# A long convolution and two MLPs in one kernel: matmuls cut into row and column tiles, and the hand-over between two stages rearranged

## The chip, the cores and the metric

The kernel runs on one core of a Trainium2 chip. A core has five engines with an instruction stream each: TensorE (PE: matmuls, and PEld: loads of the stationary operand), VectorE (DVE), ScalarE (ACT), GpSimd (POOL) and SyncE (SP). Transfers are issued from the queues of SP and ACT and run on the core's 16 DMA engines. The metric is device time in microseconds (us); of several runs the median counts.

## The reference

The input has 12480 positions and 128 channels. An implicit long convolution comes first, then two MLPs of width 2048, all in fp32:

```
h  = max(pos_emb @ w1, 0) @ w2 * exp(-0.01 * pos)     # filter, 64 -> 64 -> 128
u  = x * v
y  = irfft(rfft(u, 2S) * rfft(h, 2S), 2S)[:S]          # causal convolution over S = 12480
x1 = x * y
x2 = max(x1 @ w_in, 0)**2 @ w_out                      # first MLP
x3 = silu-like(x2 @ w_in2) @ w_out2                    # second: h * sigmoid(1.702 h)
```

## The kernel before

The Fourier transforms are matmuls with constant matrices; 12573 = 99 x 127 points are worked as 99 rows by 127. Four stages follow one another on TensorE:

- **Filter stage** (`filter_stage`): pos_emb times a block-diagonal w1, to `h`.
- **S1** (`s1_step`, L259): 48 steps of a first transform, 16 for `h` (result `G`, written to DRAM as `gd`) and 32 for `u` (result `A`, kept in SBUF). Each step has 8 matmuls whose stationary operand has 64 columns; the two halves of the output go to partitions 0 to 63 and 64 to 127.
- **S2** (`stage_s2`, L285): 99 frequencies k, in pairs p, two pairs to a group g. For a group `features` makes `fk` (4 matmuls), which ACT copies to `fs`. For a pair `spectra` makes `hk` = filter spectrum (L316: `fs` times `w2b`, a block-diagonal 128 x 256 copy of w2, 2 matmuls) and `xk` = input spectrum (L318, 2 matmuls), and ACT copies `hk` to `hc`. `product` multiplies them as complex numbers on DVE (two products `t`, L329, and a subtraction, L334) and POOL (an addition, L333). `back` transforms the product (`ob`, L342, 2 matmuls); ACT copies it to `bs` and writes it to DRAM as `bd`.
- **MLP** (`mlp`, L413): 25 tiles of up to 504 positions, 8 units to a tile and layer, 400 units in all. `unit_in` is 6 fp32r matmuls (`hin`), ACT and DVE apply the activation and split it into a high and a low part (`gh`, `gl`), and `unit_out`, four units later (LAG), is 6 matmuls (`acc`). Ahead of a tile's units its inverse transform is made: `load_b` fetches `uv` from `bd`, `combine` (L391) adds or subtracts its halves to `b`, `inverse` (L441) makes 10 matmuls into `yps`, `front_y` multiplies with x, and `split` (L428) makes `hi` and `lo`.

The weights arrive as fp64 and are converted on the chip to a high and a low fp32r part: `conversion` (L121) is 8 DVE instructions and one ACT cast for a chunk of 512 columns, and `Weights.tick` issues one step of each running conversion at a time. Of the first MLP's 8 chunks, six are converted during S2; the last two (3 and 7) are fetched near its end (ticks 44 and 46) and converted by `finish` after the last pair. The second MLP's 8 chunks are converted in the first 45 or so units.

The order of the instructions is the order in which the code is written; every engine works its own list in order. Between S2 and the first unit TensorE runs `spare`: matmuls whose result nobody reads, 9 ahead of the first tile's inverse and 2 behind it. An fp32 matmul is two records in the trace (two load and matmul pairs), an fp32r matmul is one.

Of the kernel before, what the change touches and what calls it, by code (L numbers as in the profile page):

```python
# [9 lines left out]
FP32 = mybir.dt.float32  # L10
# [4 lines left out]
ALU = mybir.AluOpType  # L15
# [12 lines left out]
D = 128  # L28
# [63 lines left out]
def conv_mlp_kernel(ctx: ExitStack, tc: tile.TileContext, xc, xt, vc, pt, w1, w2,  # L92
# [62 lines left out]
    class Weights:  # L155
# [16 lines left out]
                self.run.append(conversion(n, self.raw.pop(n), self.pool))  # L172
                next(self.run[-1])

        def finish(self):
            while self.run or self.plan:
                self.tick(1 << 30)

    class Inputs:

# [104 lines left out]
    def stage_s2(sp, mp, A, w2b, hooks, work):  # L285


        kp = tc.tile_pool(name="kp", bufs=2, space=PSUM, reuse_waits="tile")
        obp = tc.tile_pool(name="obp", bufs=2, space=PSUM, reuse_waits="tile")
        P_t, k_t, bs_t, f_t = {}, {}, {}, {}  # L290

        def pair(p):
            return min(2, N1 - 2 * p)

        with kp as kp, obp as obp:
            def features(g):


                if g >= NFK:
                    return  # L300
                n = min(FK, N1 - g * FK)
                ps = kp.tile([128, FK, 128], FP32, tag="fk", name="fk", bufs=1)
                for i in range(n):
                    k = g * FK + i
                    nc.tensor.matmul(out=ps[:, i], lhsT=h_t[k // HL][:, k % HL, :],  # L305
                                     rhs=m_t[k // 2][:, k % 2, 0, :])
                f_t[g] = sp.tile([128, FK, 128], FP32, tag="fs", name="fs", bufs=2)
                nc.scalar.copy(out=f_t[g][:, 0:n], in_=ps[:, 0:n])

            def spectra(p):  # L310
                n, m = pair(p), m_t[p]
                xk = kp.tile([128, 2, 2, D], FP32, tag="xk", name="xk", bufs=3)
                hk = kp.tile([128, 2, 2, D], FP32, tag="hk", name="hk", bufs=2)
                for j in range(n):
                    k = 2 * p + j
                    nc.tensor.matmul(out=hk[:, j], lhsT=f_t[k // FK][:, k % FK, :], rhs=w2b)  # L316
                for j in range(n):
                    nc.tensor.matmul(out=xk[:, j], lhsT=m[:, j, 0, :], rhs=A[:, 2 * p + j])  # L318
                hc = sp.tile([128, 2, 2, D], FP32, tag="hc", name="hc", bufs=2)
                nc.scalar.copy(out=hc[:, 0:n], in_=hk[:, 0:n])  # L320
                k_t[p] = xk, hc

            def product(p):
                n = pair(p)
                xk, hc = k_t.pop(p)
                t = []
                for c in range(2):
                    t.append(sp.tile([128, 2, 2, D], FP32, tag=f"t{c}", name=f"t{c}", bufs=2))
                    nc.vector.tensor_tensor(  # L329
                        out=t[c][:, 0:n], in0=xk[:, 0:n, c].unsqueeze(2).to_broadcast([128, n, 2, D]),  # L330
                        in1=hc[:, 0:n], op=ALU.mult)
                P = sp.tile([128, 2, 2, D], FP32, tag="P", name="P", bufs=3)
                nc.gpsimd.tensor_tensor(out=P[:, 0:n, 1], in0=t[0][:, 0:n, 1], in1=t[1][:, 0:n, 0], op=ALU.add)  # L333
                nc.vector.tensor_tensor(out=P[:, 0:n, 0], in0=t[0][:, 0:n, 0], in1=t[1][:, 0:n, 1],  # L334
                                        op=ALU.subtract)
                P_t[p] = P

            def back(p):
                n, m, P = pair(p), m_t.pop(p), P_t.pop(p)
                ob = obp.tile([128, 2, 2, D], FP32, tag="ob", name="ob")  # L340
                for j in range(n):
                    nc.tensor.matmul(out=ob[:, j], lhsT=m[:, j, 1, :], rhs=P[:, j])  # L342
                g, o = divmod(2 * p, HK)
                if o == 0:
                    bs_t[g] = sp.tile([128, HK, 2, D], FP32, tag="bs", name="bs", bufs=2)
                nc.scalar.copy(out=bs_t[g][:, o:o + n], in_=ob[:, 0:n])
                if o + n == HK or p == NP - 1:
# [48 lines left out]
    def load_b(bp, t):  # L396


        last = max(p[0] for p in whole(t)) // JG
        for k in range(loaded[0], last + 1):  # L400
            uv = bp.tile([N1, 2, JG, 2, D], FP32, tag="uv", name="uv", bufs=2)
            for h in range(2):
                queue = nc.scalar if t == 0 and h else nc.sync
                queue.dma_start(out=uv[:, h], in_=bd[h, k * JG:(k + 1) * JG].rearrange("j k c d -> k j c d"))
# [8 lines left out]
    def mlp(lp, cp):  # L413
# [68 lines left out]
        def front_x(t):  # L482
            split(y_t.pop(t), 0, t)
# [66 lines left out]
        for q in range(NQ + SHIFT):  # L550
            if q < NQ:
                seq.append((0, q // PAIRS, q % PAIRS))
            if q >= SHIFT:
                seq.append((1, (q - SHIFT) // PAIRS, (q - SHIFT) % PAIRS))
        for k, s, c, engine in ((0, 0, 0, nc.vector), (0, 1, 0, nc.gpsimd), (0, 0, 1, nc.vector),
                                (0, 1, 1, nc.gpsimd), (1, 0, 0, nc.vector), (1, 1, 1, nc.gpsimd),
                                (1, 0, 1, nc.vector), (1, 1, 0, nc.vector)):
            combine(k, s, c, engine)

        def spare(n):  # L560

# [2 lines left out]
                nc.tensor.matmul(out=ps[0:N1, 0:width(0)], lhsT=ci2[:, 0, :], rhs=xs[0:N1])  # L564

        xs = x_t[0][:, 0:width(0)]
        spare(9)
        front_y(0)
        spare(2)
        front_x(0)  # L570
        load_rest()
        prev = None
        work = Weights([8, 12, 9, 13, 10, 14, 11, 15], 3, 5, 3, cp)
        for n in range(len(seq) + LAG):
            work.tick(n)
            if n >= LAG:
                unit_out(*seq[n - LAG])
            if n < len(seq):
                l, t, j = seq[n]
                un = unit_in(l, t, j)  # L580
                if prev:
                    high(prev)
                gate(un)
                if prev:
                    low(prev)
                prev = un
                if l == 0:
                    if j == 0 and t + 1 < NTILE:
                        load_x(lp, t + 1)
                        load_b(bp, t + 1)  # L590
                    late = t >= SHIFT // PAIRS
                    if t == 0 and j == 2:
                        front_rest()
                    if j == 3 + late and t + 1 < NTILE:
                        front_y(t + 1)
                    if j == 5 + late and t + 1 < NTILE:
                        front_x(t + 1)
            elif prev:
                high(prev)
                low(prev)  # L600
                prev = None
        es.close()

    with tc.manual_schedule():
# [32 lines left out]
        with tc.tile_pool(name="A", bufs=1, reuse_waits="tile") as ap_, ExitStack() as mps:  # L637
            A = ap_.tile([128, N1, 2, D], FP32, name="A")
            for d in range(0, D, 4):
# [7 lines left out]
                if d // 4 == 22:  # L647
                    assert inputs.done == NXC
                    vps.close()
                    mp = mps.enter_context(tc.tile_pool(name="mh", bufs=1, reuse_waits="tile"))  # L650
                    w2b = mp.tile([128, 2 * D], FP32, name="w2b")
# [18 lines left out]
        mlp(lp, cp)  # L670


def _constants():
# [86 lines left out]
```

## Time and profile before

| | |
|---|---|
| median of 3 runs | 1419.97 us (1417.61 to 1421.13) |
| the profiled execution | 1419.01 us, span 1417.2 us, granted clock 0.993 of full |
| PE busy | 1399.3 us, 99% of the span |
| DVE, ACT, POOL busy | 1114.3 us (79%), 940.4 us (66%), 221.2 us (16%) |
| on the chain that ended last | PE 92%, DVE 4% |

The span runs from the first to the last instruction; 1.8 us lie around it. In rows of a timeline and of the chain the first number is the start in us, the second the duration in us. A matmul record's duration is modelled and longer than the distance to the next matmul, so that distance is read from the chain of waits, where a piece is as long as the engine took for it. In groups of instructions a row gives the line, engine, operation, names and shapes (for a matmul rows*columns of the stationary operand first), the count, busy us, mean ns of one, and idle time before it with what ended it. In a table of stretches the columns are the stretch, its length, busy us and count of PE, PEld, DVE, ACT and POOL, the granted TensorE clock (1.00 is 2.4 GHz, 0.50 is 1.2 GHz), the DMA engines' busy share and GB/s.

### The profile page before, as it was taken

The numbers are of one execution on the slowest core, as the hardware profiler recorded it, in microseconds if no ns is written. First come the engines' busy times: TensorE is split into PE (matmuls) and PEld (weight loads), VectorE is DVE, ScalarE is ACT, GpSimd is POOL, SyncE is SP. The second block draws the span as 40 slices with busy tenths as digits, with TensorE's granted clock in tenths as the row PEclk, the third lists the DMA queues.
The fourth block names the chain that finished last, engine by engine and source line by source line (L and its number), as shares of the span: only waits on it lengthen the run. The fifth ranks groups of instructions, "written<-read, shape, count | busy, mean of one in ns | idle before, by whom it ended". The sixth has DMA issues, their size and how long they took to land.

```text
span 1417.2 us, 17764 instructions
## 1 busy us (share of the span) xinstructions
PE 1399.3 (99%) x7018; PEld 1175.7 (83%) x7018; DVE 1114.3 (79%) x1233; ACT 940.4 (66%) x1066; POOL 221.2 (16%) x209
## 2 busy tenths in 40 slices
PE   7999999999999999999999999999999999999998
PEld 7888888788788888888888888888888888888887
DVE  7558988699887777777778777777778787777887
ACT  1654544577667767776767767777777767777776
POOL 3012222425620111111100211012101120000000
PEclk9999999899999999999999999999999999999999
DMA  9977765312200001000010000010000100000000
GB/s 248 302 247 241 242 229 195 102 60 79 68 20 8 26 20 38 25 9 20 27 38 8 27 20 26 8 38 19 27 27 8 38 19 8 8 8 1 15 15 15
DMA packets 46400, 91.34 MB, mean 64 GB/s; under 512 B 4183, under 2 KB 30604, under 8 KB 45804
## 3 DMA queue, kind: packets, MB, share of 16 engines
q1 hardware_dynamic: 36750, 64.71, 15.2%
q10 hardware_dynamic: 9566, 25.49, 4.7%
q8 instruction: 55, 0.90, 0.3%
q14 instruction: 29, 0.24, 0.1%
HBM read 64.33 MB, written 25.85 MB: 64 GB/s over the span
## 4 chain that ended last, share of the span: by engine, by line
PE 92%; DVE 4%; issue 1%; DMA 1%; ACT 1%; POOL 0%; SPq 0%; DVEq 0%; POOLq 0%; ACTq 0%
PE hin L489 12%; PE hin L490 12%; PE hin L488 12%; PE acc L489 12%; PE acc L488 12%; PE acc L490 12%; PE s L266 5%; PE yps L446 4%; PE hk L316 3%; PE xk L318 3%; PE ob L342 3%; PE fk L305 2%; DVE gl L526 1%; DVE r L250 1%; DMA uv<-bd 1%
## 5 line engine op out<-in xcount | busy, mean ns | idle before, releaser
L526 DVE TENSOR_TENSOR gl<-g,gh 128x1004 fp32r<-128x1004 f32 (+4 forms) x400 | 491.7, 1229 | 34.9 <-ACT gh L522 34.5
L506 ACT ACTIVATE g<-hin 128x1004 f32<-128x1004 f32 (+4 forms) x200 | 201.2, 1006 | 238.4 <-PE hin L490 237.9
L488 PE MATMUL acc<-gh,w 128*128 128x502 f32 (+4 forms) x800 | 313.6, 392 | 0.3 <-DVE lo L435 0.3
L488 PE MATMUL hin<-hi,w 128*128 128x502 f32 (+4 forms) x800 | 312.8, 391 | 0.0
L489 PE MATMUL acc<-gl,w 128*128 128x502 f32 (+4 forms) x800 | 311.8, 390 | 0.8 <-DVE gl L526 0.8
L489 PE MATMUL hin<-lo,w 128*128 128x502 f32 (+4 forms) x800 | 312.5, 391 | 0.0
L490 PE MATMUL hin<-hi,w 128*128 128x502 f32 (+4 forms) x800 | 311.9, 390 | 0.0
L490 PE MATMUL acc<-gh,w 128*128 128x502 f32 (+4 forms) x800 | 311.7, 390 | 0.0
L517 DVE TENSOR_TENSOR g<-hin,g 128x1004 f32<-128x1004 f32 (+4 forms) x200 | 238.7, 1193 | 50.6 <-ACT g L509 50.5
L393 POOL TENSOR_TENSOR b<-uv 99x256 f32<-99x256 f32 x127 | 158.1, 1274 | 698.4 <-DMA uv<-bd 501.0
L515 DVE CAST gh<-g 128x1004 fp32r<-128x1004 f32 (+4 forms) x200 | 142.4, 712 | 149.7 <-ACT g L507 149.6
L509 ACT ACTIVATE g<-hin 128x1004 f32<-128x1004 f32 (+4 forms) x200 | 200.1, 1001 | 75.2 <-PE hin L490 67.2
L507 ACT ACTIVATE g<-g 128x1004 f32<-128x1004 f32 (+4 forms) x200 | 208.0, 1040 | 6.4
L522 ACT CAST gh<-g 128x1004 fp32r<-128x1004 f32 (+4 forms) x200 | 202.8, 1014 | 0.4 <-DVE g L517 0.4
L488 PEld LDWEIGHTS hin<-hi,w 128*128 128x128 f32 x800 | 151.4, 189 | 33.8 <-ACT g L506 2.5
L489 PEld LDWEIGHTS acc<-gl,w 128*128 128x128 f32 x800 | 151.1, 189 | 32.0 <-DVE gl L526 2.1
L490 PEld LDWEIGHTS hin<-hi,w 128*128 128x128 f32 x800 | 151.4, 189 | 30.7
L488 PEld LDWEIGHTS acc<-gh,w 128*128 128x128 f32 x800 | 151.2, 189 | 30.8 <-DVE lo L435 0.7
L489 PEld LDWEIGHTS hin<-lo,w 128*128 128x128 f32 x800 | 151.3, 189 | 30.6 <-issue 0.5
L490 PEld LDWEIGHTS acc<-gh,w 128*128 128x128 f32 x800 | 150.8, 189 | 30.4
L329 DVE TENSOR_TENSOR t<-xk,hc 128x512 f32<-128x512 f32 (+1 forms) x100 | 63.8, 679 | 23.7 <-PE xk L318 19.5
L333 POOL TENSOR_TENSOR P<-t,t 128x256 f32<-128x256 f32 (+1 forms) x50 | 43.8, 876 | 176.8 <-DVE t L329 94.5
(56 smaller groups left out, 1032.1 us busy)
## 6 DMA issues: line engine op xcount, KB each, us to landing
uv<-bd SPq DMA_DIRECT2D x64, 198.0 KB
m<-in_c_s_dram SPq DMA_DIRECT2D x49, 256.0 KB
bd<-bs ACTq DMA_DIRECT2D x24, 512.0 KB
x<-in_xc_dram SPq DMA_DIRECT2D x16, 384.0 KB
v<-in_vc_dram SPq DMA_DIRECT2D x16, 384.0 KB
Gs<-gd ACTq DMA_DIRECT2D x10, 512.0 KB
gd<-G SPq DMA_DIRECT2D x3, 1600.0 KB
raw<-in_moe_w_in_dram SPq DMA_DIRECT2D x8, 512.0 KB
```

The source lines that it names most:

```text
L266: nc.tensor.matmul(out=ps[j, e], lhsT=src[:, d + e, j], rhs=cs1[:, half])
L393: engine.tensor_tensor(out=b[:, :, s, c], in0=uv[:, 0, :, c], in1=uv[:, 1, :, 1 - c], op=ALU.add if s != c else ALU.subtract)
L488: nc.tensor.matmul(out=out, lhsT=a, rhs=hl[0], start=first, stop=False)
L489: nc.tensor.matmul(out=out, lhsT=a, rhs=hl[1], start=False, stop=False)
L490: nc.tensor.matmul(out=out, lhsT=b, rhs=hl[0], start=False, stop=last)
L506: nc.scalar.activation(out=g, in_=ps, func=ACTF.Relu)
L507: nc.scalar.activation(out=g, in_=g, func=ACTF.Square)
L509: nc.scalar.activation(out=g, in_=ps, func=ACTF.Sigmoid, scale=1.702)
L515: nc.vector.tensor_copy(out=gh, in_=g)
L517: nc.vector.tensor_tensor(out=g, in0=ps, in1=g, op=ALU.mult)
L522: nc.scalar.copy(out=gh, in_=g)
L526: nc.vector.tensor_tensor(out=gl, in0=g, in1=gh.bitcast(FP32), op=ALU.subtract)
```

## The change

- **Row tiles in S2.** `w2` comes as two copies of its 64 rows, one above the other, instead of block-diagonal. A new function `filters` makes a whole group's `hk`: for each of 4 frequencies two matmuls with 64 rows each, one on partitions 0 to 63, one on 64 to 127, 128 columns wide, into two banks. One ACT copy of 128 x 1024 takes the place of two of 128 x 512, and in `product` one DVE multiplication of 128 x 1024 that of two of 128 x 512. `P` has two buffers instead of three.
- **Column tiles in the inverse.** Each matmul of `inverse` is cut into two with 64 columns of `b` each, into partitions 0 to 63 and 64 to 127.
- **The hand-over.** All four `uv` loads of the first tile are issued by SP (two were by ACT). The six `combine`s that tile 0 needs all run on DVE, in the order in which they are used (five were on DVE, three on POOL); the two that tile 1 needs follow on POOL behind `front_x(0)`. `spare` runs 7 instead of 9. `finish(1)` leaves one chunk (7) unconverted, and the MLP's loop converts it, one step a unit (`rest.tick`).

The diff, cut to its core (the slicing of the copies in `product` and of `w2`'s layout on the host are left out):

```
         def finish(self, left=0):
-            while self.run or self.plan:
-                self.tick(1 << 30)
+            while self.run or len(self.plan) > left:
+                self.tick(1 << 30 if len(self.plan) > left else 0)
...
+            def filters(g):
+                n = min(FK, N1 - g * FK)
+                hk = kp.tile([128, 2, FK, D], FP32, tag="hk", name="hk", bufs=1)
+                for i in range(n):
+                    for c in range(2):
+                        f = slice(c * F, (c + 1) * F)
+                        nc.tensor.matmul(out=hk[:, c, i], lhsT=f_t[g][f, i, :], rhs=w2b[f])
+                h_c[g] = sp.tile([128, FK, 2, D], FP32, tag="hc", name="hc", bufs=2)
+                nc.scalar.copy(out=h_c[g][:, 0:n], in_=hk[:, :, 0:n].rearrange("p c k d -> p k c d"))
...
-                for j in range(n):
-                    k = 2 * p + j
-                    nc.tensor.matmul(out=hk[:, j], lhsT=f_t[k // FK][:, k % FK, :], rhs=w2b)
...
+                nc.vector.tensor_tensor(out=t[:, 0:n], in0=xk[:, 0:n].unsqueeze(3).to_broadcast(full),
+                                        in1=hc.unsqueeze(2).to_broadcast(full), op=ALU.mult)
...
             for p in range(NP + 2):
+                if p < NP and p % 2 == 0:
+                    filters(p // 2)
                 if p < NP:
                     spectra(p)
...
-            work.finish()
+            work.finish(1)
...
-                queue = nc.scalar if t == 0 and h else nc.sync
-                queue.dma_start(out=uv[:, h], ...
+                nc.sync.dma_start(out=uv[:, h], ...
...
                 for c in range(2):
-                    nc.tensor.matmul(out=ps[:, o:o + w], lhsT=b[:, c, :], rhs=ci2[:, c, r:r + w],
-                                     start=(c == 0), stop=(c == 1))
+                    for d in (slice(0, D // 2), slice(D // 2, D)):
+                        nc.tensor.matmul(out=ps[d, o:o + w], lhsT=b[:, c, d], rhs=ci2[:, c, r:r + w],
+                                         start=(c == 0), stop=(c == 1))
...
-        for k, s, c, engine in ((0, 0, 0, nc.vector), (0, 1, 0, nc.gpsimd), (0, 0, 1, nc.vector),
-                                (0, 1, 1, nc.gpsimd), (1, 0, 0, nc.vector), (1, 1, 1, nc.gpsimd),
-                                (1, 0, 1, nc.vector), (1, 1, 0, nc.vector)):
-            combine(k, s, c, engine)
+        for k, s, c in ((0, 0, 0), (0, 0, 1), (0, 1, 0), (0, 1, 1), (1, 1, 0), (1, 1, 1)):
+            combine(k, s, c, nc.vector)
...
-        spare(9)
+        spare(7)
         front_y(0)
         spare(2)
         front_x(0)
+        for c in range(2):
+            combine(1, 0, c, nc.gpsimd)
         load_rest()
...
         for n in range(len(seq) + LAG):
+            rest.tick(1 << 30)
             work.tick(n)
```

On TensorE, in S2, between two `features` (`-` is the kernel before, `+` the changed one; L342 and L347 are `back`, L316 and L318 with `hk` the filter spectrum):

```order
-L342 MATMUL ob<-P,m 128x256 x2
-L316 MATMUL hk<-w2b,fs 128x256 x2
-L318 MATMUL xk<-A,m 128x256 x2
-L342 MATMUL ob<-P,m 128x256 x2
-L316 MATMUL hk<-w2b,fs 128x256 x2
-L318 MATMUL xk<-A,m 128x256 x2
+L347 MATMUL ob<-P,m 128x256 x2
+L326 MATMUL xk<-A,m 128x256 x2
+L347 MATMUL ob<-P,m 128x256 x2
+L318 MATMUL hk<-w2b,fs 128x128 x8
+L326 MATMUL xk<-A,m 128x256 x2
```

The four wide `hk` matmuls of two pairs have become eight narrow ones at one place, ahead of the even pair's `xk`.

On DVE, from the end of S2 to the first unit, in the kernel before (`w0` holds the first MLP's converted weights, `b` the combined inverse input):

```order
L144 SCALAR_TENSOR_TENSOR cm_2315<-cm_2315,cs_2305 128x512
L148 TENSOR_TENSOR w0_918<-cm_2311,w0_918 128x512
L148 TENSOR_TENSOR w0_918<-cm_2315,w0_918 128x512
L393 TENSOR_TENSOR b_2339<-uv_2336 99x2x128 x2
L393 TENSOR_TENSOR b_2343<-uv_2340 99x2x128 x3
L457 TENSOR_TENSOR y_2395<-yps_2384,xs_2176 128x492
```

and in the changed kernel:

```order
L144 SCALAR_TENSOR_TENSOR cm_2231<-cm_2231,cs_2226 128x512
L148 TENSOR_TENSOR w0_918<-cm_2231,w0_918 128x512
L400 TENSOR_TENSOR b_2252<-uv_2249 99x2x128 x4
L400 TENSOR_TENSOR b_2256<-uv_2253 99x2x128 x2
L464 TENSOR_TENSOR y_2314<-yps_2293,xs_2116 128x492
L441 TENSOR_TENSOR lo0_2320<-y_2314,hi0_2319 128x492
L131 TENSOR_SCALAR cs_2333<-raw_2162 128x512
```

One conversion instead of two ends ahead of the sums, and the other one's first step (L131) now stands behind the first tile's `lo`.

On DVE in the changed kernel, around the end of that conversion (`gl_2510`, `gl_2533` and `gl_2556` are the low parts of units 6, 7 and 8; L131, L142 and L144 belong to the second MLP's chunks):

```order
L533 TENSOR_TENSOR gl_2510<-g_2508,gh_2509 128x2x492
L142 SCALAR_TENSOR_TENSOR cm_2516<-raw_2335,cm_2516 128x512
L131 TENSOR_SCALAR cs_2539<-raw_2467 128x512
L522 CAST gh_2555<-g_2554 128x1008
L533 TENSOR_TENSOR gl_2533<-g_2531,gh_2532 128x2x492
L148 TENSOR_TENSOR w0_918<-cm_2441,w0_918 128x512
L144 SCALAR_TENSOR_TENSOR cm_2516<-cm_2516,cs_2401 128x512
```

The last write to `w0` (L148, chunk 7's low part) now stands behind unit 7's low part. Unit 6's `unit_out` is the first to read that chunk; its third matmul carries the wait:

```order
L495 MATMUL acc_2444<-gh_2509,w0_918 128x492
L496 MATMUL acc_2444<-gl_2510,w0_918 128x492 [waits DVE_49]
L497 MATMUL acc_2444<-gh_2509,w0_918 128x492 [waits DVE_49]
L495 MATMUL acc_2444<-gh_2509,w0_918 128x492
L496 MATMUL acc_2444<-gl_2510,w0_918 128x492
L497 MATMUL acc_2444<-gh_2509,w0_918 128x492
```

## Rows read from the trace of the kernel before

**Rows 1.** The page: the chain that ended last, by engine and by line

```profile
PE 92%; DVE 4%; issue 1%; DMA 1%; ACT 1%; POOL 0%; SPq 0%; DVEq 0%; POOLq 0%; ACTq 0%
PE hin L489 12%; PE hin L490 12%; PE hin L488 12%; PE acc L489 12%; PE acc L488 12%; PE acc L490 12%; PE s L266 5%; PE yps L446 4%; PE hk L316 3%; PE xk L318 3%; PE ob L342 3%; PE fk L305 2%; DVE gl L526 1%; DVE r L250 1%; DMA uv<-bd 1%
```

**Rows 2.** Busy time by stretch: S2, the hand-over, and a later stretch of slow clock

```profile
92.36:243.50 151.14, 149.98 (x784) 134.15 (x785) 130.39 (x200) 74.04 (x129) 43.77 (x50) 1.00 0.67 225
243.50:253.40 9.90, 7.86 (x21) 3.10 (x19) 7.93 (x17) 1.88 (x4) 0.76 (x1) 1.00 0.50 175
253.40:263.60 10.20, 9.90 (x30) 7.16 (x30) 4.15 (x6) 0.60 (x1) 5.12 (x8) 0.50 0.75 212
369.40:376.30 6.90, 6.69 (x19) 5.65 (x20) 3.71 (x5) 0.00 (x0) 5.15 (x7) 0.51 0.36 110
```

**Rows 3.** The chain of waits at the start of S2

```profile
90.60 1.10 PE fk L305 x8
...
94.36 0.89 PE fk L305 x8
...
100.46 0.86 PE hk L316 x4
101.32 0.86 PE xk L318 x4
```

**Rows 4.** The chain of waits: all of S1, and one tile's inverse

```profile
23.23 67.37 PE s L266 x768
...
409.68 2.21 PE yps L446 x20
```

**Rows 5.** Groups of instructions by shape: weight loads

```profile
L266 PEld LDWEIGHTS s<-cs,u 99*64 99x64 f32 x512 | 36.9, 137 | 6.9 <-DVE u L213 0.7
L305 PEld LDWEIGHTS fk<-m,Gs 128*128 128x128 f32 x198 | 26.0, 191 | 2.9 <-DMA m<-in_c_s_dram 1.3 <-issue 0.3
```

**Rows 6.** Groups of instructions by shape: DVE products

```profile
L517 DVE TENSOR_TENSOR g<-hin,g 128x1004 f32<-128x1004 f32 x88 | 105.4, 1198 | 20.1 <-ACT g L509 20.1
L329 DVE TENSOR_TENSOR t<-xk,hc 128x512 f32<-128x512 f32 x98 | 63.0, 684 | 23.7 <-PE xk L318 19.5 <-PE fk L305 2.0 <-ACT hc L320 1.7
```

**Rows 7.** Waits of PE in S2

```profile
PE fk L305 <- DMA m<-in_c_s_dram: 1.2, 1, 1.2
```

**Rows 8.** Timeline of the hand-over, all engines

```profile
243.51 7.59 PE L564 MATMUL spare<-xs,ci 99*99 99x492 f32 x18
...
246.77 0.77 SPq L404 DMA_DIRECT2D uv<-bd  x2
...
249.26 1.46 DVE L148 TENSOR_TENSOR w<-cm,w 128x512 fp32r<-128x512 f32 x2
...
249.46 0.78 ACTq L404 DMA_DIRECT2D uv<-bd  x2
...
252.57 3.36 DVE L393 TENSOR_TENSOR b<-uv 99x256 f32<-99x256 f32 x5 [1.85 <-DMA uv<-bd]
...
253.14 0.47 PE L446 MATMUL yps<-ci,b 99*128 99x99 f32 x2 [2.04 <-DVE b L393]
...
258.12 0.67 DVE L457 TENSOR_TENSOR y<-yps,xs 128x492 f32<-128x492 f32 x1 [2.19 <-PE yps L446]
...
260.40 1.36 PE L488 MATMUL hin<-hi,w 128*128 128x492 f32 x1
```

**Rows 9.** Timeline of DVE, units 7 to 9

```profile
283.00 0.42 DVE L140 TENSOR_SCALAR cm<-raw 128x512 int32<-128x512 int32 x1
283.79 0.67 DVE L515 CAST gh<-g 128x984 fp32r<-128x984 f32 x1 [0.37 <-ACT g L507]
...
287.15 1.18 DVE L526 TENSOR_TENSOR gl<-g,gh 128x984 fp32r<-128x984 f32 x1
288.24 0.69 DVE L144 SCALAR_TENSOR_TENSOR cm<-cm,cs 128x512 f32<-128x512 f32 x1
```

**Rows 10.** Timeline of PE, unit 6's `unit_out`, third matmul

```profile
287.37 0.39 PE L490 MATMUL acc<-gh,w 128*128 128x492 f32 x1
```

More of the change, by code (lines that the diff above doesn't have):

```diff
@@ L173, in tick, with finish @@
                 next(self.run[-1])
-        def finish(self):
-            while self.run or self.plan:
-                self.tick(1 << 30)
+        def finish(self, left=0):
+            while self.run or len(self.plan) > left:
+                self.tick(1 << 30 if len(self.plan) > left else 0)
     class Inputs:
@@ L289, in stage_s2 @@
         obp = tc.tile_pool(name="obp", bufs=2, space=PSUM, reuse_waits="tile")
-        P_t, k_t, bs_t, f_t = {}, {}, {}, {}
+        P_t, k_t, bs_t, f_t, h_c = {}, {}, {}, {}, {}
         def pair(p):
@@ L312, in spectra @@
                 xk = kp.tile([128, 2, 2, D], FP32, tag="xk", name="xk", bufs=3)
-                hk = kp.tile([128, 2, 2, D], FP32, tag="hk", name="hk", bufs=2)
-                for j in range(n):
-                    k = 2 * p + j
-                    nc.tensor.matmul(out=hk[:, j], lhsT=f_t[k // FK][:, k % FK, :], rhs=w2b)
                 for j in range(n):
                     nc.tensor.matmul(out=xk[:, j], lhsT=m[:, j, 0, :], rhs=A[:, 2 * p + j])
-                hc = sp.tile([128, 2, 2, D], FP32, tag="hc", name="hc", bufs=2)
-                nc.scalar.copy(out=hc[:, 0:n], in_=hk[:, 0:n])
-                k_t[p] = xk, hc
+                k_t[p] = xk
             def product(p):
                 n = pair(p)
[L325 to L334, printed above, removed]
+                xk, o = k_t.pop(p), 2 * p % FK
+                hc = h_c[2 * p // FK][:, o:o + n]
+                t = sp.tile([128, 2, 2, 2, D], FP32, tag="t", name="t", bufs=2)
+                full = [128, n, 2, 2, D]
+                nc.vector.tensor_tensor(out=t[:, 0:n], in0=xk[:, 0:n].unsqueeze(3).to_broadcast(full),
+                                        in1=hc.unsqueeze(2).to_broadcast(full), op=ALU.mult)
+                P = sp.tile([128, 2, 2, D], FP32, tag="P", name="P", bufs=2)
+                nc.gpsimd.tensor_tensor(out=P[:, 0:n, 1], in0=t[:, 0:n, 0, 1], in1=t[:, 0:n, 1, 0], op=ALU.add)
+                nc.vector.tensor_tensor(out=P[:, 0:n, 0], in0=t[:, 0:n, 0, 0], in1=t[:, 0:n, 1, 1],
                                         op=ALU.subtract)
@@ L402, in load_b @@
             for h in range(2):
-                queue = nc.scalar if t == 0 and h else nc.sync
-                queue.dma_start(out=uv[:, h], in_=bd[h, k * JG:(k + 1) * JG].rearrange("j k c d -> k j c d"))
+                nc.sync.dma_start(out=uv[:, h], in_=bd[h, k * JG:(k + 1) * JG].rearrange("j k c d -> k j c d"))
             b = bp.tile([N1, JG, 2, 2, D], FP32, tag="b", name="b", bufs=3)
@@ L411, in load_b, with mlp @@
         loaded[0] = last + 1
-    def mlp(lp, cp):
+    def mlp(lp, cp, rest):
         es = ExitStack()
@@ L650, in conv_mlp_kernel @@
                     mp = mps.enter_context(tc.tile_pool(name="mh", bufs=1, reuse_waits="tile"))
-                    w2b = mp.tile([128, 2 * D], FP32, name="w2b")
+                    w2b = mp.tile([128, D], FP32, name="w2b")
                     nc.sync.dma_start(out=w2b, in_=w2)
@@ L669, in conv_mlp_kernel @@
         split_weights(w1_, 1)
-        mlp(lp, cp)
+        mlp(lp, cp, work)
 def _constants():
@@ L738 @@
     laid['pt'] = _folded(inputs['pos_emb']).transpose(1, 3, 2, 0).reshape(2 * F, NJ, N1)
-    for name in ('w1', 'w2'):
-        f, e = inputs[name].shape
-        laid[name] = np.zeros((2, f, 2, e), np.float32)
-        for i in range(2):
-            laid[name][i, :, i] = inputs[name]
-        laid[name] = laid[name].reshape(2 * f, 2 * e)
+    f, e = inputs['w1'].shape
+    laid['w1'] = np.zeros((2, f, 2, e), np.float32)
+    for i in range(2):
+        laid['w1'][i, :, i] = inputs['w1']
+    laid['w1'] = laid['w1'].reshape(2 * f, 2 * e)
+    laid['w2'] = np.concatenate([inputs['w2']] * 2)
     given = [(n, np.ascontiguousarray(laid[n])) for n in _INS]
```

## The prediction

> **What bounds the kernel now.** I read the page first: busy time and the chain that ended last. TensorE is busy 99% of the span (the table above) and holds 92% of the chain; the MLP's `hin` and `acc` are 72% of it and are not touched. What the change touches is S1's neighbour S2 (`hk` 3%) and the inverse (`yps` 4%) [rows 1]. Second came the table by stretch. S2 (151.1 us) has PE busy 150.0 us, and DVE 130.4 us, so PE sets the time there and DVE is not far behind; between S2 and the first unit PE idles, and then runs 10.2 us at a granted clock of 0.50, which is the 1.2 GHz level [rows 2]. Third, the chain's pieces for the distance from one matmul to the next, fourth the timeline of the hand-over, fifth DVE and PE around units 6 to 9.
>
> **The change part by part.** All terms are against the profiled execution: 1419.01 us, of which 1417.2 is the span. That is 1 us under the median of 1419.97, within what a measurement of this kernel can tell; I leave the 1 us out.
>
> *Row tiles.* A group's `hk` is now 8 records at 0.86/4 = 0.216 us [rows 3], 1.73 us; 24.75 groups make 42.8 us. After, it is 16 records of half the columns. No row shows two matmuls on different rows, so the cost is bounded. If two run side by side, a pair takes what one record of 128 columns takes, 0.89/8 = 0.111 us as in `fk` [rows 3]: 8 x 0.111 = 0.89 us. If they run one after the other, it is 16 x 0.111 = 1.78 us. The nearest row is S1: 768 records in 67.37 us are 0.0877 us each [rows 4], while 198 columns at the pace of `xk` (0.216 us for 256) take 0.167 us. So S1's two halves, on different columns, do run in pairs. I take side by side.
>
> To this comes the change between a cut and an uncut array. The first `fk` behind S1 took 1.10 us where the later ones take 0.89 [rows 3], so going from tiles back to the whole array cost 0.21 us. The other direction has no clean row; between 0 and 0.21 I take 0.2. A group then costs 0.89 + 0.4 = 1.29 us, 0.44 less than now: 24.75 x 0.44 = **-10.9 us**. The Trainium skill (TensorEngine Tiling (Array Packing), Tiling Modes) says that a change of tiling mode, unlike a change of tile, drains the engine; it gives no price, and the 0.21 us agrees with it. Without it the term would be 24.75 x 0.84 = -20.8 us.
>
> DVE must keep up. Its two products of 0.684 us become one of twice the width, about 1.2 us by the nearest row, 1004 columns in 1.198 us [rows 6]. Some 0.1 us x 50 pairs go, so 125 of its 130 us stay against a stage of 140 us: 89% instead of 86%. The stage can't fall much under 130 us for this reason, and where two conversions overlap a pair may be late: **+1 us**. ACT (74 of 151 us) hides its copy. Of SP's loads of `m` one came 1.2 us late [rows 7]. It is issued when a `back` ends and needed 5 x 0.865 + 0.44 = 4.76 us later; after, 3 x 0.865 + 1.29 + 0.44 = 4.33 us: **+0.4 us**.
>
> *Column tiles.* A tile's 20 records take 2.21 us, 0.111 each [rows 4], although 99 columns stream in 0.084 us: the load of 128 columns sets the pace, as in `fk`. A load of 64 columns is 54 ns shorter (137 against 191) [rows 5], so it no longer does. At S1's pace, halved for half the columns, 40 records x 0.0439 = 1.75 us, and 0.4 us for the two changes of mode: 2.15 us, 0.06 us less, 25.4 tiles' worth: **-1.6 us**. With free changes it would be -0.46 x 25.4 = -12 us, with changes twice as dear +8.6 us.
>
> *The hand-over.* Now the first sum waits for the `uv` halves that ACT issues at 249.46, behind its casts; it starts 3.11 us later, at 252.57, and the first `hin` is at 260.40 [rows 8]. SP's first two loads go out at 246.77, when the last `bd` has landed, at 0.385 us each. With four of them there the second half of k = 0 leaves at 247.16, and its sum can start at 250.27. DVE is free by then, since one chunk is converted instead of two (those ended at 250.72). Six sums at 3.36/5 = 0.67 us end at 254.3, the last matmuls 0.4 us on, and `hin` follows after the 2.28 us that it now follows `y`: 257.0, **-3.4 us**. The two sums moved to POOL run beside this, and tile 1 needs them ten us later. Fewer `spare` cost nothing, nobody reads them; but PE then idles from 249.3 to 250.85, 1.5 us instead of 2.0. That gap may again be followed by the slow clock; now it covers 3.2 us of `hin`. If it stays away, 1.6 us are gained; if its 10.2 us lie wholly under units, 3.5 us are lost. I take no difference.
>
> *The spread conversion.* Chunk 7 is complete when its last step (L148) runs as the first DVE instruction of unit 9's turn, and unit 6's `unit_out`, in unit 10's turn, reads it with its third matmul. Now that matmul runs at 287.37 [rows 10], and unit 9's turn on DVE starts at 288.24, behind unit 7's `gl` (287.15, 1.18 us) [rows 9]. So even a DVE that lost nothing is done at 288.9: 1.5 us late. And it loses: the steps in units 3 to 6 are four of 0.42 to 0.69 us, 2.5 us, of which I let 0.8 us fall into DVE's idle gaps, two of about 0.4 us [rows 9]. That makes 1.5 + 1.7 = **+3.2 us**. Everything on PE's list stands behind the waiting matmul, so it is lost in full. SP's fetch of the second MLP's chunk 12 waits for the raw buffer until unit 5, and tile 2's `xs` and `uv` behind it; they are needed at unit 11, some 10 us on, which hides a transfer of the 3 us that `uv` takes.
>
> Sum: -10.9 + 1 + 0.4 - 1.6 - 3.4 + 3.2 = -11.3 us, 1419.0 - 11.3 = 1407.7, said as **1408 us**. Its own range is 1402 to 1413, from a change of mode between 0.15 and 0.25 us and a late chunk between 1.5 and 4 us.
>
> **The rivals.**
>
> *A: the row tiles' loads go one at a time (slower).* For: no row shows otherwise, `fk` takes 0.111 us a record with a load of 128 columns, and a tile of 64 rows still loads 128 columns; S1's loads were of 64 columns and its pace was set by streaming, so it does not tell whether full-width loads overlap. Then a group is 16 x 0.111 + 0.4 = 2.18 us, 0.45 more than now, and the term is +11.1 instead of -10.9: 1408 + 22 = 1430. It decides as soon as a pair takes over (1.73 - 0.4)/8 = 0.166 us. The Trainium skill (TensorE: Matmul & The Clock Gate, LDWEIGHTS) says that a load's time goes by its columns and not by its rows, which fits this rival; the same skill's tiling page says that different tiles load in parallel, which fits the forecast. No run here shows the one or the other for rows. Chance 0.14.
>
> *B: a load and its matmul can't be issued faster than S1 shows, 0.0877 us a record (slower).* For: no stretch in the trace is denser. Against: S1's pace is fully explained by 198 columns. Then a tile's inverse is 40 x 0.0877 + 0.4 = 3.9 us, +1.7 x 25.4 = +43, and the row tiles save nothing: about 1463. Chance 0.04.
>
> *C: the clock.* After a stall of some 2 us inside the MLP the clock was at 0.51 for 6.9 us [rows 2], which costs 3.4 us. If the late chunk brings the same, and the hand-over's slow stretch slides under the units (+3.5), it is 1408 + 7 = 1415. For: both stalls are of the size of those before. Against: in the hand-over the gap shrinks. Chance 0.16.
>
> *D: changing the mode is nearly free inside a stage.* Against it stands the 0.21 us. Then -20.8 (held to about -19 by DVE) and -12, with the rest as above: about 1389. Chance 0.08.
>
> *E: the overlap in DVE or the `m` loads eat the row tiles' gain* (the stage stays at 148 us or more): about 1416 to 1419. Against: DVE has 15 us of idle time in it, and one wait for `m` in 50. Chance 0.05.
>
> **How the numbers follow.** The forecast has 0.53, its range 1402 to 1413. Within 0.3% (about what a measurement can tell from no change) means 1415.7 to 1424.2. Faster: the forecast 0.52, D 0.08, more than half of C 0.1, and 0.01 of E, 0.71. The same: the rest of C and E, and the lower edge of A, 0.12. Slower: A, B and a misjudged price of the mode change, 0.17. The range of 1395 to 1430 holds the forecast, C, E and the lower half of A, and leaves out D, B and the upper half of A, 0.2.
>
> **What would show it.** In the changed kernel's chain a group's 16 `hk` records should take 1.2 to 1.4 us (A: over 2) and S2 about 141 us; a tile's 40 `yps` records 1.7 to 1.8 us with a gap of some 0.2 us at either side (B: 3.5); the first `hin` about 13.5 us after the first `spare`, against 16.9; and a wait of `acc` for DVE's `w` of 1.5 to 4 us, once, at unit 6. The forecast is wrong if S2 is not shorter by at least 6 us, or if the inverse is longer than now.

## The result, and the profile after

The changed kernel takes **1407.29 us** (median of 4 runs, 1404.03 to 1412.15) against 1419.03 for the kernel before in the same comparison: ratio 0.992, 95% interval 0.9901 to 0.9938. The profiled execution has a span of 1406.2 us, 11.0 less than before. The next table has each kernel's median and, from its one profiled execution, the stages: from the first matmul of one stage to the first of the next (the end of the span for the last). The runs that follow below stand in it too. Executions of one kernel differ by some 10 us at most, and the shorter ones mostly have the higher mean granted clock (the changed kernel: 1404.0 us at 0.996, 1406.6 at 0.995, 1408.0 at 0.993, 1412.2 at 0.991), so a stage can be off by some us from what the median execution would show. Ratios compare with the kernel before on the same chip.

| kernel | median us | S1 | fk to hk | S2 | hand-over | MLP |
|---|---|---|---|---|---|---|
| before | 1419.0 | 67.3 | 1.8 | 151.2 | 16.9 | 1156.8 |
| after | 1407.3 | 69.4 | 1.8 | 141.1 | 13.8 | 1156.7 |
| e3 columns only | 1413.0 | 65.5 | 1.8 | 151.4 | 16.4 | 1148.9 |
| e4 rows only | 1413.8 | 70.4 | 2.6 | 143.9 | 16.8 | 1151.9 |
| e7 hand-over only | 1416.6 | 67.8 | 1.8 | 151.8 | 13.9 | 1156.5 |
| e1 no spread | 1403.3 | 69.7 | 1.8 | 140.3 | 13.8 | 1150.9 |
| b0, e1 again | 1406.4 | 70.7 | 2.7 | 144.8 | 14.0 | 1148.7 |
| e2 rows in turn | 1421.7 | 68.7 | 1.8 | 152.9 | 13.8 | 1154.7 |
| e5 twice the changes | 1418.6 | 69.3 | 1.8 | 150.9 | 14.1 | 1154.9 |
| e6 two steps | 1411.2 | 71.1 | 2.7 | 144.2 | 13.9 | 1156.3 |
| e8 free places | 1409.1 | 67.5 | 1.8 | 143.9 | 13.9 | 1157.2 |
| b3 = e1 + spares | 1405.4 | 69.7 | 2.7 | 142.5 | 12.1 | 1152.5 |
| b1 = e1 + places | 1401.8 | 68.4 | 1.8 | 141.4 | 14.1 | 1148.9 |
| b2 = e1 + both | 1399.1 | 68.6 | 1.8 | 142.9 | 12.2 | 1152.8 |

So S2 gave 10.05 us and the hand-over 3.07; the MLP, in which the column tiles lie, came out level, and S1, in which no matmul was edited, lost 2.1.

The stretches of the changed kernel that answer to [rows 2] (busy us and records of PE, PEld, DVE, ACT, POOL, then granted clock): S2, the hand-over in two pieces, and a slow stretch at unit 6.

```profile
94.53:235.63 141.10, 139.66 (x982) 118.74 (x983) 125.25 (x150) 70.38 (x104) 48.43 (x50) 1.00 0.73 244
235.63:243.23 7.60, 5.95 (x16) 2.19 (x14) 4.13 (x9) 1.25 (x3) 0.00 (x0) 1.00 0.55 205
243.23:249.45 6.22, 6.22 (x44) 4.13 (x45) 4.01 (x8) 0.60 (x1) 3.06 (x4) 0.52 0.62 204
277.65:284.48 6.83, 5.29 (x13) 4.28 (x14) 4.47 (x7) 1.35 (x2) 0.00 (x0) 0.50 0.05 21
```

PE still fills S2 (139.7 of 141.1 us). DVE lost only 5 us there, and is now busy 89% of the stage. The last stretch is new.

The chain of waits of the changed kernel (start, length, what), one group of S2, answering to [rows 3]:

```profile
98.51 1.09 PE hk L318 x16
99.60 1.06 PE xk L326 x4
100.66 0.89 PE fk L305 x8
101.55 0.86 PE ob L347 x4
102.42 0.86 PE xk L326 x4
103.28 0.86 PE ob L347 x4
104.14 1.09 PE hk L318 x16
```

Sixteen records take 1.09 us, 8 pairs at 0.111 and 0.20 more at the entry; the `xk` behind them takes 1.06 where the other takes 0.86, 0.20 more on the way out. The group costs 1.29 us, to the hundredth what the forecast took. In the trace the two loads of a pair start 6 to 7 ns apart and pairs follow at 111 to 112 ns: the row tiles run side by side, loads included.

The same view at a tile's inverse, answering to the second of [rows 4], first of the kernel before, then of the changed one:

```profile
409.45 0.23 PE hin L490
409.68 2.21 PE yps L446 x20
411.88 0.25 PE acc L488
412.14 0.23 PE acc L489
```

```profile
402.05 0.22 PE hin L497
402.27 1.84 PE yps L453 x40
404.12 0.42 PE acc L495
404.54 0.22 PE acc L496
```

From the start of the `yps` piece to the end of the first `acc` piece a tile of before took 2.21 + 0.25 = 2.46 us and one of the changed kernel 1.84 + 0.42 = 2.27 (from 402.27 to 404.54): -0.19 us. In the trace the two records of a pair start 7 ns apart and pairs follow at 0.085 us.

The hand-over in the timeline (all engines; start, duration, what), answering to [rows 8]:

```profile
235.63 5.94 PE L569 MATMUL spare<-xs,ci 99*99 99x492 f32 x14
238.86 1.65 SPq L410 DMA_DIRECT2D uv<-bd  x4
242.66 1.43 DVE L400 TENSOR_TENSOR b<-uv 99x256 f32<-99x256 f32 x4 [2.65 <-DMA uv<-bd]
243.23 3.65 PE L453 MATMUL yps<-ci,b 99*64 99x99 f32 x40 [1.66 <-DVE b L400]
246.93 0.67 DVE L464 TENSOR_TENSOR y<-yps,xs 128x492 f32<-128x492 f32 x1 [1.35 <-PE yps L453]
249.45 1.21 PE L495 MATMUL hin<-hi,w 128*128 128x492 f32 x1
```

The first sum starts 7.03 us behind the first `spare` (9.06 before), the first `hin` 13.82. PE waits 1.66 us for `b`, and from 243.5 on the clock is at the 1.2 GHz level for 6.8 us (0.52 on the mean of the stretch above), so that 40 `yps` take 3.65 us.

PE's waits of the changed kernel from 240 to 420 us (total, times, longest), and the chain of waits around unit 6:

```profile
PE acc L497 <- DVE w L148: 3.7, 1, 3.7
PE acc L496 <- DVE gl L533: 2.7, 3, 2.3
```

```profile
272.57 1.72 DVE gl L533
274.29 1.15 DVE cm L142
275.44 0.87 DVE cs L131
...
277.36 1.18 DVE gl L533
278.54 0.61 DVE w L148
279.15 0.04 issue
279.19 0.78 PE acc L497
279.97 0.41 PE acc L495
```

The forecast wait is there, at unit 6: `acc` stands 4.1 us for the last step of the spread conversion. Matmuls behind it go at 0.41 us instead of 0.23, and the clock is at 0.50 for 6.8 us. The first 1.5 us of these, from 277.65 to 279.19, still fall into the standstill.

### The profile page after: what moved, and what is told of

Its sections match the earlier page's. It is cut to its first block, busy times and chain, and to the rows that moved or that the text cites. A ratio compares the mean times of both kernels' runs of the same rounds, so it can differ in the third digit from the quotient of the medians.

```text
span 1406.2 us, 19109 instructions
## 1 busy us (share of the span) xinstructions
PE 1382.8 (98%) x7720; PEld 1143.8 (81%) x7720; DVE 1114.9 (79%) x1184; ACT 937.2 (67%) x1041; POOL 223.6 (16%) x208
## 4 chain that ended last, share of the span: by engine, by line
PE 89%; DVE 5%; DMA 4%; issue 1%; ACT 1%; SPq 0%; DVEq 0%; ACTq 0%
PE acc L495 12%; PE hin L496 12%; PE hin L497 12%; PE hin L495 12%; PE acc L496 12%; PE acc L497 12%; PE xk L326 3%; PE yps L453 3%; PE ob L347 3%; PE s L266 2%; PE hk L318 2%; DVE gl L533 2%; PE fk L305 2%; DMA x<-in_xc_dram 1%; DMA v<-in_vc_dram 1%
## 5 line engine op out<-in xcount | busy, mean ns | idle before, releaser
L496 PEld LDWEIGHTS acc<-gl,w 128*128 128x128 f32 x800 | 151.2, 189 | 35.2 <-DVE gl L533 5.3
L497 PEld LDWEIGHTS hin<-hi,w 128*128 128x128 f32 x800 | 151.4, 189 | 30.7
L496 PEld LDWEIGHTS hin<-lo,w 128*128 128x128 f32 x800 | 151.2, 189 | 30.6 <-issue 0.5
L338 POOL TENSOR_TENSOR P<-t 128x256 f32<-128x256 f32 (+1 forms) x50 | 48.4, 969 | 164.1 <-DVE t L335 132.2
L335 DVE TENSOR_TENSOR t<-xk,hc 128x1024 f32<-128x1024 f32 (+1 forms) x50 | 60.3, 1205 | 15.4 <-ACT hc L320 11.1
```

The costliest lines, as they stand in the source:

```text
L335: nc.vector.tensor_tensor(out=t[:, 0:n], in0=xk[:, 0:n].unsqueeze(3).to_broadcast(full), in1=hc.unsqueeze(2).to_broadcast(full), op=ALU.mult)
L496: nc.tensor.matmul(out=out, lhsT=a, rhs=hl[1], start=False, stop=False)
L497: nc.tensor.matmul(out=out, lhsT=b, rhs=hl[0], start=False, stop=last)
```

## The experiments

**e1: the changed kernel without the spread conversion.**

```
-            work.finish(1)
+            work.finish()
...
-            rest.tick(1 << 30)
```

> The changed kernel, but with both last chunks converted ahead of the MLP as before (nothing is spread). Theory 1 (the late chunk 7 makes PE wait at unit 6, and the wait brings the slow clock): the changed kernel's profile shows a distance of 4.11 us at that matmul and 6.8 us at half clock behind it; both go, 3.9 + 3.4 = 7.3 us, and the hand-over grows by at most 0.5 us, since the conversions then end at about the time at which the uv land: about 1400 us. Theory 2 (the spread is what shortens the hand-over, since DVE is the one that is late there): the hand-over gets 3 us longer again, 13.8 to about 17 us, and only 4 us are gained: about 1403 us. If the wait at unit 6 stays, both are wrong.

1403.30 us (6 runs), ratio 0.9889 (0.9868 to 0.9910). The hand-over stays at 13.80 us, the MLP loses 5.9 us, and among PE's waits after the hand-over that for `w` is gone:

```profile
PE acc L496 <- DVE gl L533: 2.7, 3, 2.3
PE yps L453 <- DVE b L400: 2.0, 2, 1.7
PE yps L453 <- POOL b L400: 0.2, 1, 0.2
```

Theory 1 holds by stage: leaving the chunk to the MLP buys nothing in the hand-over, where DVE waits 2.65 us for `uv` anyway, and costs 5.9 us later, less than the 7.3 that theory 1 said. The total is that of theory 2, but its hand-over of 17 us did not come. A second series of this kernel (b0 below) is 3 us higher, so by time alone the step is not larger than its scatter.

**e3: column tiles alone.** The kernel before, with only the edit of `inverse`.

> The kernel before with the column tiles in the inverse alone. Theory 1 (two column tiles run side by side, loads of 64 columns overlap, and the changes of mode cost less than I put them): a tile's inverse takes 0.2 us less including its edges, as in the changed kernel's trace (0.317 + 1.845 + 0.333 against 0.227 + 2.15 + 0.312 us), 25 x 0.195 = 4.9 us: about 1414 us. Theory 2 (PE's gain is given back by the other engines, DVE above all, which is full while weights are converted): under 2 us are gained.

1412.97 us, ratio 0.9964 (0.9948 to 0.9980); before had a median of 1419.76 beside it. Per tile the distances are those of the changed kernel. The MLP is 7.9 us shorter, but not by 25.4 tiles at 0.19: followed from unit to unit (the table in the next section), 3.9 us are a stall of before at 366 us that did not come, and the column tiles gave about 4, nearly all behind unit 48. From unit 16 to unit 32 both kernels take 49.1 to 49.3 us; VectorE, which converts weights there, is busy 48.6 of before's 49.2 us, and a shorter inverse buys nothing. The total is near theory 1, in part by that stall.

**e4: row tiles alone.** The changed kernel with everything else as before.

> The kernel before with the row tiles in S2 alone (w2 stacked, filters, the wide product). Theory 1 (S2 stays bound by PE and gets shorter by 10 us, from 151.1 to 141.1 us, as in the changed kernel; the rest stays): about 1409 us, the hand-over at 16.9 us and no wait at unit 6. Theory 2 (part of the 10 us was the conversion that left S2's end): S2 gets shorter by 8 us or less.

1413.82 us, ratio 0.9965 (0.9947 to 0.9982): 4 us less gain than theory 1 said. S2 is 7.3 us shorter, which is theory 2's number, but not for its reason: the groups take their 1.29 us here too once the clock is at full. What its profile lost against theory 1 lies at the end of S1 and the start of S2 (PE's timeline):

```profile
94.08 1.95 PE L305 MATMUL fk<-m,Gs 128*128 128x128 f32 x8 [2.19 <-DMA Gs<-gd]
96.70 2.08 PE L318 MATMUL hk<-w2b,fs 64*128 64x128 f32 x16 [0.68 <-ACT fs L308]
```

PE waits 2.19 us for `Gs`, and the clock is then low for 6.8 us, which makes the start of S2, up to the second `xk`, 2.0 us longer than in the changed kernel. SP's timeline says why `Gs` is late, first of the kernel before, then of the changed one:

```profile
81.46 3.70 SPq L276 DMA_DIRECT2D m<-in_c_s_dram  x2
85.20 0.43 SPq L283 DMA_DIRECT2D Gs<-gd  x1
```

```profile
81.97 6.73 SPq L276 DMA_DIRECT2D m<-in_c_s_dram  x2
88.74 0.43 SPq L283 DMA_DIRECT2D Gs<-gd  x1
```

The second `m` load leaves 3.5 us later, and `Gs` stands behind it. In the changed kernel it leaves when VectorE's last fold of the input ends (the L213 at 87.66 in DVE's timeline, 0.69 us long), before when the last but one ended (84.12, 0.69 us):

```profile
87.66 0.69 DVE L213 TENSOR_TENSOR u<-x 99x512 f32<-99x512 f32 x1
```

```profile
84.12 0.69 DVE L213 TENSOR_TENSOR u<-x 99x512 f32<-99x512 f32 x1
```

The cause is a place in SBUF. `w2b` was halved from 1024 to 512 bytes a partition, and everything allocated behind it moved down by 512. In the programs as they were built the second `m` began at byte 133600 in the kernel before, exactly where the last input chunk's `x` (129504 to 133600) ends; at 133088 it reaches into that chunk. Over all profiles: PE waits 1.2 to 2.8 us for `Gs` in the eight with the halved `w2b` and the old order of places, and not at all in the six without (before, e3, e7, and with other places e8, b1, b2).

**e7: the hand-over alone.** The kernel before with SP's loads, the six sums on DVE, 7 pairs of `spare`; both chunks converted ahead.

> The kernel before with the hand-over's loads and sums alone: all four uv loads on SP, six sums on DVE, seven spare matmuls; both chunks are converted ahead as before. Theory 1 (the uv issues behind ACT's casts were late; DVE is not): the hand-over, 16.9 us, becomes about 14 us, total 3 us less: about 1416 us. Theory 2 (DVE, full of conversions until 7.2 us after the first spare matmul, then has six sums instead of five): the hand-over stays over 16 us and the total within 1 us of before.

1416.57 us, ratio 0.9985 (0.9972 to 0.9998); hand-over 13.9 us. Theory 1 holds. The three parts alone give -6.8, -5.9 and -3.2 us, together -15.9, which is 1403.9 and close to e1, the changed kernel without the spread. Stalls that come in one profile and not in another are in these numbers, so the closeness proves little.

**e2: the row tiles not alternating.**

```
-                for i in range(n):
-                    for c in range(2):
+                for c in range(2):
+                    for i in range(n):
```

> The changed kernel, with the hk matmuls of a group issued as all of one row tile and then all of the other; work and operands are the same. Theory 1 (two row tiles run side by side only where their matmuls are neighbours in the queue): 16 records one after another at 0.111 us and 0.4 us for the change of tile shape make 2.18 us a group in place of 1.29, so 25 groups cost +22 us: about 1429 us, and S2 about 163 us. Theory 2 (the pace does not hang on the order, a record is 0.055 us by itself): 1407 us, S2 141 us.

1421.74 us (1416.91 to 1425.67), ratio 1.0016 (1.0000 to 1.0032); S2 152.9. Neither theory has the number. A group in the chain:

```profile
110.66 1.64 PE hk L318 x16
112.30 1.06 PE xk L326 x4
```

1.64 us, 0.55 more than alternating, where theory 1 said 0.89 more. The order matters, but less: the records of one row tile follow at 0.11 us, and the trace has the second tile's first three matmuls beside the first tile's fifth to eighth. So they started although matmuls of the other tile, ahead of them in the order, were still to come.

**e5: twice as many changes between row tiles and the whole array.** `filters` makes two of a group's four frequencies at a time.

```
-                if p < NP and p % 2 == 0:
-                    filters(p // 2)
+                if p < NP:
+                    filters(p // 2, p % 2)
```

> The changed kernel with each group of 16 hk matmuls cut into two of 8 (one ahead of each pair's xk), so S2 changes between row tiles and the whole array twice as often, with the same matmuls; ScalarE copies in halves. Theory 1 (a change there and back costs TensorE 0.3 to 0.4 us): 25 more of them, +7 to +10 us, 1414 to 1417 us, S2 about 149 us. Theory 2 (it is nearly free): within 1 us of 1407, S2 141 us.

1418.60 us, ratio 0.9995 (0.9983 to 1.0008), 1.6 above theory 1's range; S2 150.9, +9.8. By the stage theory 1 holds: 0.39 us for each of 25 more round trips. In the chain:

```profile
114.79 0.65 PE hk L322 x8
115.43 1.06 PE xk L332 x4
```

Eight records are 4 x 0.111 = 0.44 us and 0.20 for the entry; the 0.20 on the way out is again in `xk`. The Trainium skill (TensorEngine Tiling (Array Packing), Tiling Modes) says that a change of tiling mode drains the engine. It gives no price; measured here it is 0.39 us there and back.

**e6: two steps of the spread conversion in a unit.** A second `rest.tick(1 << 30)` in the loop.

> The changed kernel, but two steps of the spread conversion are taken in each unit, so that its last chunk is ready some two units earlier. Theory 1 (acc at unit 6 waits because that conversion is too late on VectorE, and the slow TensorE clock after it follows from this wait): the wait of 4.1 us and the slow stretch at 277 us are both gone, 1400 to 1403 us. Theory 2 (VectorE has no room in these units, and the wait only moves to gl or y): 1406 to 1408 us.

1411.20 us, ratio 0.9933 (0.9914 to 0.9952). The wait for `w` is gone, but PE's waits from 240 to 420 us now begin with `gl`, 5.6 us in place of 2.7, and the slow stretch still comes (3.4 us):

```profile
PE acc L496 <- DVE gl L533: 5.6, 5, 2.3
PE yps L453 <- DVE b L400: 2.3, 2, 1.9
```

The MLP is 0.4 us shorter: what unit 6 no longer loses is lost in the units ahead of it (28.0 us for the first eight, 21.3 in the changed kernel), and at unit 16 both are level within 0.5 us. Theory 2: VectorE has no room in these units, so its work can only come late in one place or another. The total is above the forecast of both theories; the profiled execution also has the slow clock at the start of S2, after a wait of 2.3 us for `Gs`.

**e8: the places of `m` in rising order**, so that the first two `m` and `Gs` lie on memory that is free early.

```
-        m_t[p] = mp.tile([128, 2, 2, 128], FP32, tag="m", name="m", bufs=7)
+        m_t[p] = mp.tile([128, 2, 2, 128], FP32, tag=f"m{p % 7}", name="m", bufs=1)
```

> The changed kernel with the seven places of m given out in rising order. Halving w2b moved m's second place 512 bytes down, over the end of an input chunk that the last fold reads, so that in the changed kernel the second m load (and Gs behind it on SP) waits for that last fold, 3.5 us later than before; here the first two m and Gs lie on memory that is free earlier. Theory 1 (S1 is 2 us longer for this): fk starts at 89 to 91 us of the span and not 92.7, the total is 1404 to 1405.5 us. Theory 2 (S1's length is chance of the DMA): 1407 us, fk at 92 to 93.

1409.13 us, ratio 0.9920 (0.9905 to 0.9935): no gain in the total, so theory 1 fails there. The mechanism is confirmed all the same (SP's timeline, and PE's):

```profile
81.60 0.82 SPq L276 DMA_DIRECT2D m<-in_c_s_dram  x2
82.52 0.38 SPq L283 DMA_DIRECT2D Gs<-gd  x1
```

```profile
91.00 1.16 PE L305 MATMUL fk<-m,Gs 128*128 128x128 f32 x8
```

`Gs` leaves 6.2 us earlier and `fk` starts at 91.00 without a wait, inside the forecast 89 to 91. But in this execution S2 then waited 3.6 us for later `m` loads, 1.1 in the changed kernel, and was 2.8 us longer, which is more than the 1.9 us that S1 gained.

**b0, b3, b1, b2: what is best.** All without the spread; b3 and b2 have `spare(9)` for `spare(7)`, b1 and b2 the places of e8.

> The changed kernel without the spread conversion (it is finished ahead of the MLP), on one chip with its variants. From its run before: 1403 us. A check of that level, 1401 to 1405.

> The changed kernel without the spread conversion and with 9 in place of 7 pairs of spare matmuls ahead of the first tile's yps. Theory 1 (the slow TensorE clock of 6.8 us in the hand-over follows from the 1.7 us in which TensorE waits for b; two pairs of 0.85 us fill it): no slow stretch at 244 us, yps' 40 records in 2 to 3 us and not 3.6, the first hin 1 us earlier and the first twelve hin at full pace, 1401 to 1402 us. Theory 2 (the clock falls for another reason, or the end of the hand-over hangs on VectorE and ScalarE): 1403, first hin 13.8 us after the first spare.

> The changed kernel without the spread conversion and with the m places in rising order. Theory 1 (S1 ends 2 us earlier, but S2 then waits longer for the m that are already loaded as fast as they come, as in the run with the spread): 1402 to 1404 us, S1 and S2 together as long as without it. Theory 2 (the longer waits for m in that run were chance): 1401 us, S2 140.5 to 141.

> All three: no spread conversion, the m places in rising order, 9 pairs of spare matmuls. If both gains hold they add up to 1399 to 1400.5 us; if only that of the clock, 1401 to 1402; if neither, 1403.

On one chip: b0 1406.44 (ratio 0.9896, 0.9878 to 0.9914), b3 1405.36 (0.9901, 0.9884 to 0.9919), b1 1401.84 (0.9871, 0.9854 to 0.9888), **b2 1399.08** (0.9865, 0.9851 to 0.9879). The intervals of b1 and b2 lie wholly below that of the changed kernel, but overlap each other: which of the two is better stays open. b0 missed its level: its profiled execution has a wait of 2.8 us for `Gs` and the slow clock behind it, as b3's has (2.2 us), and with places free (b1, b2) there is neither. So it is the places that the times show here: b1 and b2 have a median of 1399.7 us over nine executions, b0 and b3 of 1406.0 over twelve. With the spread conversion (e8) they showed nothing. Between b1's theories its profile does not decide: S1 and S2 together are as long as in e1 (211.6 and 211.8 us) and 6.5 us shorter than in b0. The added `spare` do what theory 1 of b3 said in the hand-over, but its total, 1405.4, is not the 1401 to 1402 it gave. The stretch from the first `spare` to the first `hin` in b0 and in b2:

```profile
242.25:256.26 14.01, 11.47 (x59) 5.46 (x58) 11.09 (x23) 2.47 (x5) 3.00 (x3) 0.84 0.59 202
```

```profile
237.24:249.40 12.16, 11.43 (x64) 5.24 (x62) 10.39 (x23) 2.46 (x5) 1.81 (x2) 1.00 0.55 190
```

The clock stays at full and 1.85 us go. At the next tile, whose sums POOL has not ready, more than that comes back in this profile: PE waits 3.0 us for them in b2 (0.2 in e1), the clock falls for 3.4 us at 262, and the first eight units take 26.2 us against 22.0 in b0. In b3 the wait is 1.0 us and they take 22.2.

```profile
PE yps L453 <- POOL b L400: 3.0, 4, 1.2
```

So what the added `spare` are worth in the total stays open: neither b3 against b0 nor b2 against b1 is a difference that the intervals can tell.

## Why the prediction was right, point by point

The forecast was 1408 and the time is 1407.3. That it is so close is luck: single terms were off by up to 3 us, one was missing, and they happened to cancel. The mechanisms of the forecast were right in the main, with the exceptions below.

- **Row tiles, -10.9, with +1 for DVE and +0.4 for `m`:** measured -10.05 in S2. The pair at 0.111 us and the 0.4 us for both changes of mode are in the chain, and e5 measured the 0.4 apart. DVE cost 0.4 us (one product late, at the stage's end); `m` loads came late by 1.1 us, as before (1.2), so the +0.4 did not come. Some 0.5 us stay without a name. Rival A is false: it would have shown over 2 us for 16 records. Its argument, that a full-width load is as long for 64 rows as for 128, holds (187 and 190 ns on the mean) but decides nothing, since the loads of the two row tiles overlap. The Trainium skill (TensorEngine Tiling (Array Packing), Tiling Modes) says that different tiles can load and multiply in parallel. The trace agrees: the loads of a pair start 6 to 7 ns apart. The halfway step of e2 shows what would have happened without alternating.
- **Column tiles, -1.6:** by the chain -0.19 a tile, three times the 0.06 of the forecast. The term is a small difference of two large ones, and each was a little off: pairs follow at 0.085 us and not at 2 x 0.0439, the changes of mode cost 2.27 - 20 x 0.085 - 0.225 (one `acc`) = 0.35 us and not 0.4, and the uncut inverse took 2.23 us (2.46 - 0.23) and not 2.21. What also failed is the multiplication by 25.4: the gain came only where TensorE sets the pace, so the MLP got about 4 us of the 4.8. Rival B (0.0877 a record, 3.5 us for the 40) is false.
- **Hand-over, -3.4:** measured -3.07, its order as told. The first sum came 0.27 us later than worked out (7.03 against 6.76). The slow clock stayed, but 6.8 us long and not 10.2, and less of it fell on units: 1.1 us gained behind the hand-over, where the forecast took no difference. With more `spare` the hand-over itself is 1.85 us shorter (b2), which that profile lost again at the next tile.
- **Spread conversion, +3.2:** the wait is where it was put, and 3.9 us beyond a matmul's distance, at the upper end of the 1.5 to 4 given. What failed is leaving out what follows: the slow clock for 6.8 us, of which 5.3 fall on matmuls. From unit 8 to unit 16 the changed kernel takes 30.3 us and e1 23.9, so the whole costs 6.4 us and buys nothing. That is the mechanism of rival C, which had its first condition (a stall of that size inside the MLP brings the slow clock) right and the price a little high (3.4 against 2.5 us); its second condition, the hand-over's slow stretch under the units, did not come, nor did its 1415.
- **Not foreseen: S1, +2.1.** The prediction took S1 as untouched. The halved `w2b` moved the places of `m`, a load came to wait for a later reader, and `Gs` behind it on SP's queue: 1.43 us of the 2.1. The rest (0.3 is a wait for `u`) has no cause shown. In e4, e6, b0 and b3, where the wait for `Gs` was 2.2 to 2.8 us, the slow clock came with it.
- **Rivals D and E:** both false. A change of mode and back costs 0.4 us in S2, and S2 did shorten.

In the profiles S2, the hand-over and S1 add up to -10.05 - 3.07 + 2.1 = -11.0 us, which is all that was measured, so the MLP's terms cancel among themselves. Its time from the first `hin` of one unit to the first `hin` of another (us) shows where:

| units | before | e4 rows only | e3 columns only | after | e1 no spread |
|---|---|---|---|---|---|
| 0 to 8 | 22.4 | 21.2 | 22.1 | 21.3 | 21.8 |
| 8 to 16 | 24.1 | 24.1 | 23.9 | 30.3 | 23.9 |
| 16 to 32 | 49.1 | 49.2 | 49.2 | 49.3 | 49.2 |
| 32 to 48 | 52.1 | 48.2 | 48.1 | 50.4 | 50.5 |
| 48 to the end | 1009.0 | 1009.2 | 1005.5 | 1005.4 | 1005.4 |

The changed kernel gains 1.1 us in the first row (hand-over's slow clock) and 3.6 in the last (column tiles), loses 6.2 in the second (the spread conversion), and gains 1.6 in the fourth, which no run ties to the change. There, two different stalls come in some profiles and not in others. In before and e7 the next tile's `yps` waits for POOL's sums, in the changed kernel, e1, e6, e8 and b3 an `acc` waits 1.9 to 2.3 us for DVE's `gl`; in e3, e4, e2, e5, b0, b1 and b2 neither comes. Before's waits from 236 to 420 us have the first kind:

```profile
PE yps L446 <- POOL b L393: 1.7, 3, 1.2
```

With the slow clock that follows it the first costs 3.9 us (before against e4, in whose MLP nothing was edited) and the second 2.4 (e1, 50.5, against b0, the same kernel, 48.1); in e6 and e8 no slow clock follows. What decides whether one comes stays open.

## What to carry to other kernels

Cutting matmuls into tiles pays by pairs that run side by side less a fixed price for each change between cut and whole array, so collect the cut matmuls in one place and alternate the tiles. A tile that gets smaller moves the places of all that is allocated behind it: compare what each early load waits for, and look at what stands behind it on its queue. Work moved off the critical path into a stretch where its engine is full is not hidden, and work saved on TensorE in such a stretch buys nothing. A stall is priced together with the slow clock that follows it, as far as that falls on matmuls.

## What the runs showed of the hardware

- Two row tiles of 64 rows with loads of 128 columns run side by side: 0.111 us a pair in fp32, loads 6 to 7 ns apart. A load for 64 rows is hardly shorter than one for 128 (187 and 190 ns). Issued one tile after the other, 16 records took 1.64 us and not 1.09: a part still overlaps.
- A change from the whole array to row tiles and back cost 0.39 us (e5; in the chain 0.20 at either side); for column tiles between fp32r matmuls it was about 0.35 us both ways together.
- The start of S2 with the halved `w2b` in the old order of places: in four profiles PE waited 1.2 to 1.4 us for `Gs` and the granted clock stayed at 1.0; in four it waited 2.2 to 2.8 us and the clock fell to 0.5 for 6.8 us. In the hand-over of the twelve profiles without the added `spare` a wait of 1.6 to 2.0 us was followed by the slow clock; in b2 and b3 the longest wait was 0.5 us, and the clock stayed at 1.0 up to the first `hin`. Inside the MLP a wait of 1.9 to 2.3 us for `gl` was followed by the slow clock in the changed kernel, e1 and b3 and not in e6 and e8.
